# Local attention results moved into token tiles in pieces of a multiple of 16 rows and a remainder

## The chip, the cores and the metric

The kernel runs on one core of one Trainium2 chip. The metric is the device time of the core in microseconds (us). TensorE (PE) does the matrix products, VectorE (DVE), ScalarE (ACT) and GpSimd (POOL) the elementwise work, and SyncE (SP) issues every DMA of this kernel, one after the other in a fixed order; the transfers themselves run on the core's 16 DMA engines.

## The reference

Shapes: batch 8, 8 heads, 576 positions, head dimension 64; the feed-forward layer goes from 512 to 2048 and back. All in float32.

```python
# pooled attention: q, k, v averaged over groups of 4 positions, softmax over 144 positions
out_up = np.repeat(sm_attn(q_d, k_d, v_d), 4, axis=2)
# local attention: each position sees those less than 4 away
mask = np.abs(pos[:, None] - pos[None, :]) < 4
out_local = softmax(np.where(mask, scale * q @ k.T, -1e9)) @ v
x = (out_up + out_local), heads side by side          # 8 x 576 x 512
xn = (x - mean(x)) / sqrt(var(x) + 1e-6) * g_ln
return x + relu(xn @ w_ch1) @ w_ch2
```

## The kernel before, in words

The 4608 tokens (8 x 576) are 36 tiles `x` of 128 rows by 512. Two tiles make a chunk; there are 18 chunks, and each runs through the whole feed-forward layer on PE (`ffn`, L984 on): 8 pairs of hidden blocks, each pair 24 matmuls of "up" (L996, `h`) and 12 of "down" (L1019, `acc`). Products are made from a high and a low float32r part of each factor, so every product is done three times. The weights are loaded once, in 64 loads (L347, L352), and split into high and low parts by ACT and DVE (L359 to L383) in the first 150 us.

**Local attention** (`local`, L405 to L664) is done in 40 windows, 5 for each batch element. A window takes 116 output positions: two halves ("par") of NQ = 58 positions, each half with 64 keys. A window loads q, k and v (L419, L437; the first 7 windows, which are turned by PE, with L428 and L443), PE makes scores (L540), DVE masks them, ACT takes exponentials, PE turns them (`lt`, L575) and multiplies by v (`lv`, L596), and DVE divides into the window's result `xl` (L612).

**The moves.** `xl` has other rows on other partitions than the tiles `x`, so it is moved there by DMAs from SBUF to SBUF. L635 to L643 cut each half's 58 rows at the tiles' edges (every 128 tokens) into moves. A move of a window from the eighth on is two DMAs, one for each half of the heads (L662), with m partitions of 4 x 64 elements; in windows 5 and 6 it is one DMA of m rows of 512 (L659). Most of the first batch element's results are gathered by PE without a move (L884); two small moves remain at L956. In all there are 92 moves of two DMAs and 8 of one.

**The norm.** `load_up` (L865) loads the pooled result of a tile into `up`. POOL adds it to `x` (`plus`, L896) when every move into the tile has landed. DVE takes mean and variance (`st`, L904 to L907), POOL the root (L910), DVE normalises (`xn`, L914), PE turns (`px`, L923), and ACT and DVE split the turned tile into `xh` (L930) and `xlo` (L940), the inputs of the chunk's "up" matmuls.

**What sets the order.** A planner in the kernel (`Plan`, L23 to L115) lists all tasks with an engine, a cost, a due time and the buffers they take and give. It plays them through in Python while the program is built and fixes the order of every engine's instructions. At run time each engine works through its list in that order and waits where its inputs are not there. A move counts in the plan as one task of SP, with a cost of 1.52 us for two DMAs, a landing allowance LAT of 2.5 us behind it, and the buffer of `xl` comes free behind the window's last move:

```python
t = add("SP", 0.76 if by_pe else 1.52, move, outs, due + 1.0, take=() if n in piece else U,
        give=U if e == len(moves) - 1 else (), lag=LAT, kb=116)
```

Most buffers (`xl`, `x`, `up`, `xh`, `xlo`, `hh`, `hl`, weights, q and k) are the same pool of 88 units (NU). An instruction that first writes a unit waits for the last instruction or DMA that used it, whatever that was for.

Of the kernel before, what the change touches and what calls it, by code (L numbers as in the profile page):

```python
# [139 lines left out]
def attention_then_ffn(  # L140
# [258 lines left out]
    def window_start(w, par):  # L399
        return min(max(NQ * (2 * w + par) - (FACTOR - 1), 0), S - 64)  # L400
# [4 lines left out]
    def local(i):  # L405
# [230 lines left out]
        for par in range(2):  # L636
            s0 = NQ * (2 * w + par)
            n = min(NQ, S - s0)
            t, r0 = b * S + s0, s0 - window_start(w, par)
            while n:  # L640
                m = min(n, P - t % P)
                moves.append((t // P, t % P, r0, m, par))
                t, r0, n = t + m, r0 + m, n - m  # L643
        if own:
# [417 lines left out]
    for i in range(NPB * NWIN):  # L1062
        local(i)
    for b in range(B):
        pooled(b)
    for i in range(NPB * NWIN, B * NWIN):
        local(i)
# [48 lines left out]
```

## Time and profile before

| what | value |
|---|---|
| times of three runs | 1081.28, 1079.04, 1079.87 us; median 1079.87 |
| profiled execution: span from first to last instruction | 1080.9 us (no other time is given for it) |
| span against the median | 1.0 us longer |
| busy: PE, PEld, DVE, ACT, POOL | 96%, 86%, 47%, 29%, 25% |
| mean granted TensorE clock | 0.989 of full speed |
| DMA | 104.34 MB, mean 97 GB/s |

Span and runs agree within the runs' own spread. Busy shares are averages over the whole span; what a stretch waits for is read from its own rows. SP's issuing is not counted as busy; it is read from the timeline of the SP queue, where a row gives the start, the length and the number of merged issues.

### The profile page before, as it was taken

How to read it: one execution, taken by the hardware profiler on the slowest of the kernel's cores; microseconds unless marked ns; L12 is line 12 of the kernel's file. 1: busy time of each engine (PE TensorE's matmuls, PEld its weight loads, DVE VectorE, ACT ScalarE, POOL GpSimd, SP SyncE). 2: the span in 40 equal slices, each digit the busy share in tenths (PEclk: the TensorE clock that was granted, in tenths of full speed). 3: DMA queues.
4: the chain of work that ended last, by engine and by line, in shares of the span. 5: the costliest groups of instructions: out<-in, count | busy, mean ns of one | idle time of the engine just before them, and what ended most of it. 6: DMA issues, size and time to landing. Idle time of an engine off the chain costs nothing.

```text
span 1080.9 us, 23774 instructions
## 1 busy us (share of the span) xinstructions
PE 1040.3 (96%) x9290; PEld 933.6 (86%) x9290; DVE 511.9 (47%) x1309; ACT 312.7 (29%) x852; POOL 266.2 (25%) x285
## 2 busy tenths in 40 slices
PE   8987999989989999999999999999979999999998
PEld 8875898978879898989898989898968988888997
DVE  7699954434243535345344443645424353543211
ACT  5675633222222322132222221223212222222110
POOL 4234454314004221141213231142311400100000
PEclk9999899989999999999999999999999999999999
DMA  7798554625333443344343435252533333300000
GB/s 155 211 270 235 121 147 112 144 61 120 82 88 89 99 97 79 65 92 107 82 110 77 109 69 125 47 137 51 126 87 76 69 74 74 85 10 30 9 20 20
DMA packets 289296, 104.34 MB, mean 97 GB/s; under 512 B 237945, under 2 KB 276089, under 8 KB 289185
## 3 DMA queue, kind: packets, MB, share of 16 engines
q1 hardware_dynamic: 289185, 102.83, 40.2%
q8 instruction: 73, 1.20, 0.5%
q14 instruction: 38, 0.31, 0.1%
HBM read 82.58 MB, written 11.80 MB: 87 GB/s over the span
## 4 chain that ended last, share of the span: by engine, by line
PE 78%; DMA 9%; DVE 5%; SPq 4%; issue 2%; ACT 1%; POOL 1%; DVEq 0%; ACTq 0%; POOLq 0%
PE h L996 33%; PE acc L1019 32%; PE gv L802 3%; DMA s<-in_moe_w_ch_dram 2%; PE lv L596 2%; PE ls L540 2%; DMA x<-xl 2%; PE gs L766 2%; PE lt L575 1%; SPq L419 1%; PE px L923 1%; PE gt L785 1%; SPq L662 1%; DVE cva L370 1%; SPq L428 1%
## 5 line engine op out<-in xcount | busy, mean ns | idle before, releaser
L1019 PE MATMUL acc<-hi,hl 128*128 128x512 f32 x576 | 239.1, 415 | 10.2 <-DVE hl L1007 8.5
L1019 PE MATMUL acc<-lo,hh 128*128 128x512 f32 x576 | 228.5, 397 | 0.0
L1019 PE MATMUL acc<-hi,hh 128*128 128x512 f32 x576 | 226.8, 394 | 0.0
L1007 DVE SCALAR_TENSOR_TENSOR hl<-h,hh 128x512 fp32r<-128x512 f32 x144 | 98.9, 687 | 242.8 <-ACT hh L1003 222.8
L1003 ACT ACTIVATE hh<-h 128x512 fp32r<-128x512 f32 x144 | 86.1, 598 | 433.5 <-PE h L996 379.7
L996 PE MATMUL h<-xh,lo 128*128 128x256 f32 x1152 | 193.5, 290 | 0.0
L996 PE MATMUL h<-xlo,hi 128*128 128x256 f32 x1152 | 185.6, 284 | 0.0
L996 PE MATMUL h<-xh,hi 128*128 128x256 f32 x1152 | 185.6, 283 | 0.0
L996 PEld LDWEIGHTS h<-xh,lo 128*128 128x128 f32 x1152 | 169.4, 190 | 17.6 <-POOL lo L383 0.2
L996 PEld LDWEIGHTS h<-xlo,hi 128*128 128x128 f32 x1152 | 159.4, 192 | 0.0
L996 PEld LDWEIGHTS h<-xh,hi 128*128 128x128 f32 x1152 | 159.1, 192 | 0.0
L896 POOL TENSOR_TENSOR x<-x,up 128x512 f32<-128x512 f32 x32 | 41.2, 1289 | 376.8 <-DMA x<-xl 264.5
L1019 PEld LDWEIGHTS acc<-hi,hl 128*128 128x128 f32 x576 | 110.1, 191 | 27.5 <-DVE hl L1007 11.4
L1019 PEld LDWEIGHTS acc<-hi,hh 128*128 128x128 f32 x576 | 109.2, 190 | 25.3
L1019 PEld LDWEIGHTS acc<-lo,hh 128*128 128x128 f32 x576 | 110.3, 191 | 12.7
L930 ACT ACTIVATE xh<-px,gain 128x128 fp32r<-128x128 f32 x144 | 44.3, 367 | 79.5 <-PE px L923 43.6
L940 DVE SCALAR_TENSOR_TENSOR xlo<-px,gain,xh 128x128 fp32r<-128x128 f32 x144 | 43.0, 344 | 38.3 <-ACT xh L930 26.1
L904 DVE BATCH_NORM_STATS2 st<-x 128x6 f32<-128x512 f32 x32 | 22.1, 690 | 69.9 <-POOL x L896 68.7
L1027 DVE SCALAR_TENSOR_TENSOR x<-acc,x 128x512 f32<-128x512 f32 x36 | 24.3, 683 | 35.5 <-PE acc L1019 35.3
L546 DVE TENSOR_TENSOR ls<-ls,mask 128x256 f32<-128x256 f32 x66 | 27.0, 424 | 27.3 <-PE ls L540 22.3
L779 ACT ACTIVATE ag<-gs,gmx 96x144 f32<-96x144 f32 x96 | 28.8, 373 | 35.1 <-DVE gmx L771 33.1
L802 PEld LDWEIGHTS gv<-vd,agt 72*72 72x72 f32 x512 | 37.1, 145 | 1.5
(195 smaller groups left out, 1152.7 us busy)
## 6 DMA issues: line engine op xcount, KB each, us to landing
s<-in_moe_w_ch_dram SPq DMA_DIRECT2D x64, 256.0 KB
vwin<-in_v_dram SPq DMA_DIRECT2D x160, 64.0 KB
out_dram<-x SPq DMA_DIRECT2D x36, 256.0 KB
qr<-in_q_dram SPq DMA_DIRECT2D x264, 32.0 KB
kr<-in_k_dram SPq DMA_DIRECT2D x264, 32.0 KB
up<-ud SPq DMA_DIRECT2D x28, 256.0 KB
x<-xl SPq DMA_DIRECT2D x66, 58.0 KB
ud<-od SPq DMA_DIRECT2D x32, 72.0 KB
```

What stands on the lines that cost most here:

```text
L546: nc.vector.tensor_add(x.ps[n], x.ps[n], mask.unsqueeze(1).broadcast_to([P, NPAIR, 64]))
L779: nc.scalar.activation(y.a[:, c], y.ps[:, c], AF.Exp, scale=POOLED_SCALE, bias=y.mx[:, c : c + 1])
L802: nc.tensor.matmul(y.pv[:, qh, h2], lhsT=y.at[kh][:, h2, qh * GH : (qh + 1) * GH], rhs=vd[:, kh, 2 * pr + h2], start=kh == 0, stop=kh == 1,)
L896: nc.gpsimd.tensor_add(xt[n], xt[n], x.up)
L904: nc.vector.bn_stats(st, x.up if by_pe else xt[n])
L930: nc.scalar.activation(xh[c][i][:, k, j * P : (j + 1) * P], pxt[n][:, kc], AF.Copy, scale=gain[:, kc : kc + 1])
L940: nc.vector.scalar_tensor_tensor(out=xlo[c][i][:, k, ts], in0=pxt[n][:, kc], scalar=gain[:, kc : kc + 1], in1=xh[c][i][:, k, ts].bitcast(F ...
L996: nc.tensor.matmul(ph[c, p][:, fi], lhsT=wt[:, kc], rhs=xx[kc // 2][:, kc % 2], start=n == 0, stop=n == 3 * KC - 1)
L1003: nc.scalar.activation(hh[c, p], ph[c, p], AF.Relu)
L1007: nc.vector.scalar_tensor_tensor(out=hl[c, p].rearrange("p c t -> p (c t)"), in0=ph[c, p].rearrange("p c t -> p (c t)"), scalar=0.0, in1=h ...
L1019: nc.tensor.matmul(acc[c][j], lhsT=lt[:, fi, ts], rhs=rt, start=p == 0 and fi == 0 and n == 0, stop=p == NPR - 1 and fi == 1 and n == 2,)
L1027: nc.vector.scalar_tensor_tensor(out=x, in0=acc[c][j], scalar=1.0 + 2.0**-23, in1=x, op0=ALU.mult, op1=ALU.add)
```

## The change

One line is added to the loop that cuts a half's rows into moves: a piece of m rows becomes the largest multiple of 16 that is not over m; what is left is cut again in the next turn of the loop. A piece under 16 rows stays as it is.

```diff
             while n:
                 m = min(n, P - t % P)
+                m = m // 16 * 16 or m
                 moves.append((t // P, t % P, r0, m, par))
                 t, r0, n = t + m, r0 + m, n - m
```

So 58 rows become 48 and 10; 54 become 48 and 6; 34 become 32 and 2; 16 and 48 stay one piece. Moves with two DMAs go from 92 to 168, that is from 184 DMAs to 336; those with one DMA from 8 to 14. The bytes are the same. Each move is a task of the plan with the cost, the allowance and the release above, so the planner finds another order for all engines. Lines below L641 have a number higher by one in the changed kernel.

**SP, before tile 7's last moves.** `x7` is tile 7, `xl8` the result of window 8, `raw` a load for pooled attention, `kr10` and `qr10` keys and queries of window 10. Before:

```order
L700 DMA raw5v1_3028<-in_v_dram 72x4x256
L419 DMA kr10_3034<-in_k_dram 32x8x32 x4
L419 DMA qr10_2969<-in_q_dram 32x8x32 x4
L825 DMA ud2_2687<-od4_1_3082 72x2x128
L419 DMA kr10_3034<-in_k_dram 32x8x32 x4
L700 DMA raw6q0_3140<-in_q_dram 72x4x256
L700 DMA raw6k0_3143<-in_k_dram 72x4x256
L662 DMA x7_2883<-xl8_3136 58x4x64 x2
L662 DMA x7_2883<-xl8_3136 42x4x64 x2
L662 DMA x8_3175<-xl8_3136 16x4x64 x2
```

The same place in the changed kernel:

```order
L701 DMA raw5v1_3088<-in_v_dram 72x4x256
L826 DMA ud2_2709<-od4_1_3086 72x2x128
L419 DMA qr10_3016<-in_q_dram 32x8x32 x4
L701 DMA raw6q0_3146<-in_q_dram 72x4x256
L663 DMA x7_2931<-xl8_3142 48x4x64 x2
L663 DMA x7_2931<-xl8_3142 10x4x64 x2
L663 DMA x7_2931<-xl8_3142 32x4x64 x2
L663 DMA x7_2931<-xl8_3142 10x4x64 x2
L663 DMA x8_3212<-xl8_3142 16x4x64 x2
```

Eight loads of `kr10` and one of `raw6k` have moved from ahead of tile 7's moves to behind them, and the tile takes eight DMAs in place of four.

**ACT, chunk 13.** `xh13_0` and `xh13_1` are the two halves of the chunk's high part, `px26` and `px27` its turned tiles; in brackets are the semaphores for which an instruction waits (DMAHW: landings of DMAs). Before:

```order
L930 ACTIVATE xh13_0_10420<-px26_10404,gain_75 128x128 [waits PE_49,Activation_49]
L930 ACTIVATE xh13_0_10420<-px26_10404,gain_75 128x128
L930 ACTIVATE xh13_1_10438<-px26_10404,gain_75 128x128 [waits DMAHW4_49,DMAHW5_49,DMAHW1_49,DMAHW6_49,DMAHW0_49,DMAHW7_49,DVE_49,Activation_49]
L930 ACTIVATE xh13_1_10438<-px26_10404,gain_75 128x128
L930 ACTIVATE xh13_0_10420<-px27_10468,gain_75 128x128 [waits PE_49]
```

In the changed kernel:

```order
L931 ACTIVATE xh13_0_10550<-px26_10532,gain_75 128x128 [waits PE_49]
L931 ACTIVATE xh13_0_10550<-px26_10532,gain_75 128x128
L931 ACTIVATE xh13_1_10571<-px26_10532,gain_75 128x128 [waits DVE_49]
L931 ACTIVATE xh13_1_10571<-px26_10532,gain_75 128x128
L931 ACTIVATE xh13_0_10550<-px27_10602,gain_75 128x128 [waits PE_49]
```

`xh13_1` no longer waits for six DMA landings. In the same way `xlo9_0` (chunk 9) and `xlo14_0` (chunk 14) lose theirs on DVE. Over the program, the splits into `xh` and `xlo` that wait for a DMA landing go from 17 to 12; some of the 12 stand at chunks where none stood before (`xh7_0`, `xh7_1`).

**SP, among the weight loads.** `s2_13` is a weight block of the second matrix, `xl6` the result of window 6. Before:

```order
L700 DMA raw2v0_1699<-in_v_dram 72x4x256
L659 DMA x5_1315<-xl6_1693 58x512
L659 DMA x5_1315<-xl6_1693 18x512
L659 DMA x6_1741<-xl6_1693 40x512
L352 DMA s2_13_0_1760<-in_moe_w_ch2_dram 128x512
L352 DMA s2_13_1_1761<-in_moe_w_ch2_dram 128x512
```

In the changed kernel:

```order
L437 DMA vwin3_79<-in_v_dram 64x4x64 x4
L660 DMA x5_1328<-xl6_1695 48x512
L660 DMA x5_1328<-xl6_1695 10x512
L660 DMA x5_1328<-xl6_1695 16x512
L660 DMA x5_1328<-xl6_1695 2x512
L660 DMA x6_1762<-xl6_1695 32x512
L660 DMA x6_1762<-xl6_1695 8x512
L701 DMA raw2v1_1783<-in_v_dram 72x4x256
L352 DMA s2_13_0_1785<-in_moe_w_ch2_dram 128x512
L352 DMA s2_13_1_1786<-in_moe_w_ch2_dram 128x512
```

Six DMAs stand ahead of `s2_13` in place of three, and one load of `raw2v` has come between.

## Rows read from the trace of the kernel before

**Rows 1.** The page: busy engines (part 1), shares of the chain that ended last (part 4).

```profile
PE 1040.3 (96%) x9290; PEld 933.6 (86%) x9290; DVE 511.9 (47%) x1309; ACT 312.7 (29%) x852; POOL 266.2 (25%) x285
...
PE h L996 33%; PE acc L1019 32%; PE gv L802 3%; DMA s<-in_moe_w_ch_dram 2%; PE lv L596 2%; PE ls L540 2%; DMA x<-xl 2%; PE gs L766 2%; PE lt L575 1%; SPq L419 1%; PE px L923 1%; PE gt L785 1%; SPq L662 1%; DVE cva L370 1%; SPq L428 1%
```

**Rows 2.** Busy time by stretch: stretch, PE, PEld, DVE, ACT, POOL, clock, DMA share, GB/s.

```profile
600.00:700.00 100.00, 100.00 (x939) 89.99 (x938) 47.62 (x127) 25.25 (x67) 21.09 (x22) 1.00 0.38 80
700.00:800.00 100.00, 100.00 (x908) 89.98 (x908) 42.69 (x108) 23.83 (x61) 28.13 (x29) 1.00 0.44 103
```

**Rows 3.** Timeline of PE after 200 us, instructions after a pause: start, length, [pause <-releaser].

```profile
235.36 1.12 PE L575 MATMUL lt<-ident,la 128*128 128x128 f32 x4 [4.99 <-ACT la L570]
...
303.42 0.66 PE L923 MATMUL px<-ident,xn 128*128 128x128 f32 x4 [2.77 <-DVE xn L914]
...
583.18 0.66 PE L923 MATMUL px<-ident,xn 128*128 128x128 f32 x4 [1.98 <-DVE xn L914]
...
810.08 1.11 PE L923 MATMUL px<-ident,xn 128*128 128x128 f32 x4 [5.78 <-DVE xn L914]
...
868.83 0.66 PE L923 MATMUL px<-ident,xn 128*128 128x128 f32 x4 [1.21 <-DVE xn L914]
```

**Rows 4.** Chain that ended last, before the last three pauses: start, length, what.

```profile
575.55 4.91 DMA x<-xl
...
802.83 5.25 DMA x<-xl
...
808.30 0.63 ACT xh L930 x2
...
862.65 4.41 DMA x<-xl
```

**Rows 5.** Busy time by stretch while only moves are under way.

```profile
804.50:805.00 0.50, 0.00 (x0) 0.00 (x0) 0.29 (x1) 0.00 (x0) 0.50 (x2) 1.00 0.16 36
```

**Rows 6.** Busy time by stretch at the lower clock.

```profile
807.40:814.40 7.00, 4.32 (x15) 3.75 (x16) 4.61 (x12) 3.06 (x10) 0.00 (x0) 0.51 0.26 71
234.10:240.90 6.80, 5.54 (x19) 4.84 (x20) 1.69 (x3) 3.39 (x13) 0.00 (x0) 0.50 0.22 34
```

**Rows 7.** Timeline of the SP queue: start, length, line, merged issues.

```profile
104.83 2.40 SPq L659 DMA_DIRECT2D x<-xl  x3
...
219.49 7.91 SPq L662 DMA_DIRECT2D x<-xl  x6
...
571.56 5.18 SPq L662 DMA_DIRECT2D x<-xl  x6
```

**Rows 8.** Issues by line: count, min/median/max ns, first and last start us.

```profile
L662 SPq DMA_DIRECT2D x<-xl x184: 605/787/2176, 194.5 to 1001.6; - x184
...
L419 SPq DMA_DIRECT2D qr<-in_q_dram x264: 311/448/1813, 114.7 to 932.0; - x132
L419 SPq DMA_DIRECT2D kr<-in_k_dram x264: 311/448/1857, 116.8 to 934.0; - x132
...
L437 SPq DMA_DIRECT2D vwin<-in_v_dram x132: 595/615/1601, 98.5 to 907.7; - x132
```

**Rows 9.** Chain that ended last, before the pause at 235.36 us.

```profile
224.33 3.24 DMA x<-xl
...
227.73 1.30 POOL x L896
```

**Rows 10.** Timeline of DVE at L904: start, length, [idle before <-releaser].

```profile
229.05 0.69 DVE L904 BATCH_NORM_STATS2 st<-x 128x6 f32<-128x512 f32 x1 [10.55 <-POOL x L896]
...
296.67 0.69 DVE L904 BATCH_NORM_STATS2 st<-x 128x6 f32<-128x512 f32 x1 [7.73 <-POOL x L896]
...
674.86 0.69 DVE L904 BATCH_NORM_STATS2 st<-x 128x6 f32<-128x512 f32 x1 [6.16 <-POOL x L896]
...
803.07 0.69 DVE L904 BATCH_NORM_STATS2 st<-x 128x6 f32<-128x512 f32 x1 [10.53 <-POOL x L896]
```

**Rows 11.** Waits: engine line <- releaser: us in total, times, longest us.

```profile
POOL x L896 <- DMA x<-xl: 264.5, 19, 28.0
...
SPq L419 <- DVE cva L370: 3.0, 1, 3.0
```

## The prediction

> **What bounds the kernel now.** I read the page first, then stretches, then what ends each pause of PE. PE is busy for 96% of the span, and two thirds of the chain that ended last are its feed-forward products [rows 1]. In whole stretches PE never pauses, though moves run there too [rows 2]. So a late move costs nothing by itself. It costs where it makes PE pause, and where the pause is followed by a lower granted clock.
>
> After 200 us there are five pauses of over 1 us, 16.7 us in all [rows 3]. Following each back along the chain gives two kinds.
>
> *Kind A*, at 583, 810 and 868 us: 1.98 + 5.78 + 1.21 = 8.97 us. Ahead of each the chain shows a move of 4.4 to 5.3 us from its issue on [rows 4]. The instruction behind the move is not one that needs the tile: it is a write of `xh` or `xlo`. These take a unit that was `xl`, and must wait until the move has read it. At 810 us ACT writes the second half of `xh` at 808.30, when the move issued at 802.83 has landed, and DVE and PE stand behind it.
>
> *Kind B*, at 235 us: 4.99 us. Tile 7 is added up at 227.73, when a move issued at 224.33 has landed [rows 9]. DVE stood at `st` for 10.55 us [rows 10], and with it the window whose `la` PE needed. The move was late since SP reached it late: its six issues began at 219.49 [rows 7], behind the loads that the order shows.
>
> The pause at 303 us (2.77) I leave in both kernels. Two pauses bring a granted clock of one half (1.2 GHz in place of 2.4): PE worked 4.32 us so after the pause at 810 and 5.54 us after that at 235 [rows 6]. Half of that is lost: 2.2 and 2.8 us.
>
> **The change, part by part.** *How a move runs.* While only moves of 58 and 46 rows are under way, the DMA share is 0.16, that is about 2.5 of 16 engines [rows 5]. The Trainium skill (DMA: Bandwidth & Descriptors, "Why a DMA increments its semaphore by 16 and not by 1") says that a DMA is spread over the largest number of engines, up to 16, that divides its outermost size: 2 for 58 and 46, 16 for 48 and 32, 10 for 10. The trace agrees for 58 and 46; that 48 rows use all 16 no row before the change shows. By that rule the landings below would lie at their lower end, and the third that I take for the remaining waits would fall to nothing: 1072.5.
>
> *What a window pays.* Take the window with pieces of 24, 34 and 58 rows. Before: six issues from 571.56, 5.18 us long or 0.86 each [rows 7], and the last landing at 575.55 + 4.91 = 580.46 [rows 4], 8.9 us after the first issue. Afterwards: 16, 8, 32, 2, 48, 10, twelve issues. The last is issued 11 x 0.86 = 9.5 us after the first. Its landing is not in the trace. It lies between its own issue (0.86) and 3.24 us, a 42-row move behind slow ones [rows 9]: 10.3 to 12.7 us after the first issue. I take 11.5, nearer the middle because no slow piece is ahead. So the `xl` buffer comes free about 2.6 us **later** than before, not earlier; a window of 58 and 58 (eight issues, 6.0 us and then 0.86 to 3.24) comes out about even.
>
> *What the plan does with it.* The code allows 1.52 us a move and 2.5 us for the landing. For this window that was 3 x 1.52 + 2.5 = 7.1 us against 8.9 measured: the plan gave the buffer away 1.8 us too early, which is kind A. Afterwards it allows 6 x 1.52 + 2.5 = 11.6 us, about what I expect. The order bears it out: `xh13_1`, `xlo9_0` and `xlo14_0`, the three writes behind kind A, no longer wait for a landing. So **A goes: -8.97 - 2.2 = -11.1 us** (bounds 0 and -11.1). But 12 splits still wait for a landing, some at new places. Before, 17 such waits cost 11.1 us, 0.65 each; 12 at that price are 7.8 us. As the allowance now covers the landing I take a third: **+2.6** (bounds 0 and +7.8).
>
> *B.* The order puts nine loads behind tile 7's moves: eight at 0.448 [rows 8] and one like them, about 4.4 us with the gaps. It adds four issues ahead of the tile's last landing: 4 x 0.86 = 3.4. So the tile is whole about 1.0 us sooner; had the six issues taken 0.86 each in place of 7.91 / 6 = 1.32, it would be 3.7. I take 2.5 us of the pause and half of the clock's 2.8: **-3.9** (bounds 0 and -7.8).
>
> *Weights, before 150 us.* At 104.83 three moves take 2.40 us, 0.80 each [rows 7]; now six stand ahead of `s2_13`: +2.4 us, and two more pieces at an earlier place, +1.6. SP waits 3.0 us for DVE soon after [rows 11], which can hide most of it. Without that cover it is 4.0. I take half: **+2.0** (bounds 0 and +4.0).
>
> *SP from 194 to 1001 us.* 152 more issues of 0.787 us are 120 us in 807. The q, k and v loads and the moves alone take 528 x 0.448 + 132 x 0.615 + 184 x 0.787 = 463 us there [rows 8], so the queue goes from 57% to 72% by these alone, and gaps, pooled loads and stores come on top. Per tile (32 in all) it is 3.8 us more of issuing. POOL waits 19 times for moves [rows 11], mostly at no cost; PE feels it where DVE already stands at `st` for over 6 us, at four places [rows 10]. If each gets 2.8 us later, PE pays 11.2 us. The planner moves loads back to make up, as at tile 7, so I take two of four: **+5.6** (bounds 0 and +11.2).
>
> Sum: -11.1 + 2.6 - 3.9 + 2.0 + 5.6 = -4.8 us. From the span of 1080.9 us that is 1076.1, and the median of the runs is 1.0 us below the span: **1075.1 us**. What a measurement of this kernel can tell from no change is about 0.2%, 2.2 us.
>
> **Rivals.**
>
> *SP becomes what PE waits for (slower).* Each tile's moves land later by the extra issues and the planner's shifts do not make up. For it: in the window above the last landing is 2.6 us later at equal start. Against it: stretches without any pause [rows 2]. It decides from about 2.8 us at the four places of [rows 10]: 11.2 + 4.0 from the weights, with A gone but paid back by new waits of the same size: 1080.9 + 15.2 - 1.0 = 1095.1; with half of that, 1087.5. I call it 1090. The Trainium skill has a rule on this side (DMA: Bandwidth & Descriptors, "Rules for kernel authors"): many small transfers are to be joined into one, as under 64 KB the overhead rules; a piece of 58 KB is here cut into 48 and 10. On the issue side the trace agrees: a move's issue costs 0.787 us whatever its rows.
>
> *It only moves the waits (no change).* The three pauses go, the 12 waits and SP give them back: 1079.9. For it: at equal start no window's buffer is free sooner.
>
> *The spread is not set by the row count.* Then 48 rows land no faster than 58 and the split is pure issue: A stays, 1080.9 + 5.6 + 2.0 - 1.0 = 1087.5. Against it: rows 5, where three issues of 46 and 58 rows keep so few engines busy.
>
> *All gains, no cost:* 1080.9 - 11.1 - 7.8 - 1.0 = 1061.0. For it: everything added lies on SP, which is not PE.
>
> **How the numbers follow.** The forecast 1075.1 with its all-gains end: 0.46; waits only moved: 0.16; SP bound: 0.34; spread not by row count: 0.04. Faster by over 0.2%: 0.46; within: 0.16; slower: 0.34 + 0.04 = 0.38. The range goes from 1060, the all-gains case, to 1093, most of the slower rival; what lies outside is the rival's far end. Both signs have much of the chance: the forecast's own range is 1061 to 1078.
>
> **What would show it.** Right: no pause of PE ending in a wait for `xh13`, `xlo9` or `xlo14`; moves of 48 and 10 rows landing within 2 to 3 us of their issue; the clock at full speed around 810 us; a DMA share well over 0.16 while only moves run. Wrong: SP issuing without a gap over 40 us and more, POOL's waits for moves over 264.5 us in total with DVE's waits at `st` growing beyond 7 us at more than four tiles, or PE pausing for q and k loads. If the time is slower although A's pauses are gone, the term for SP is what I sized wrongly.

## The result and the profile after

| | before | changed |
|---|---|---|
| median of the runs | 1079.72 us (4 runs, 1079.04 to 1081.28) | 1070.38 us (4 runs, 1069.24 to 1071.28) |
| ratio, 95% interval | | 0.9905 [0.9891, 0.9919] |
| profiled execution: span | 1080.9 us | 1067.5 us (its own time: 1069.24) |

The changed kernel is **9.3 us faster**; 4.8 us were forecast. The two profiles lie 13.4 us apart. In the four runs of the changed kernel the time is 1.7 to 1.8 us above the span; if the same holds before, its profiled execution took some 1082.6 us, 2.9 above its median, and that of the changed kernel 1.1 below: 13.4 - 4.0 = 9.4.

The page of the changed kernel, parts 1 and 4 [rows 1]: PE is busy for as long as before, in a shorter span, and SP's issues of moves are no longer among the shares of the chain that the page lists.

```profile
PE 1040.7 (97%) x9318; PEld 934.7 (88%) x9318; DVE 506.9 (47%) x1305; ACT 317.2 (30%) x868; POOL 266.4 (25%) x285
...
PE h L997 36%; PE acc L1020 35%; PE gv L803 3%; PE lv L596 2%; PE gs L767 2%; DMA s<-in_moe_w_ch_dram 2%; PE ls L540 2%; PE lt L575 2%; PE gt L786 1%; PE px L924 1%; DMA x<-xl 1%; DVE cva L370 1%; PE ex L885 1%; PE gq L740 1%; SPq L419 1%
```

Busy time in the first 200 us and in the 800 after them (columns as in [rows 2]), of before:

```profile
0.00:200.00 200.00, 180.83 (x1745) 162.00 (x1746) 149.69 (x365) 105.35 (x292) 85.34 (x99) 0.97 0.68 174
200.00:1000.00 800.00, 782.33 (x7065) 702.24 (x7065) 346.84 (x916) 197.32 (x540) 178.99 (x184) 0.99 0.38 85
```

and of the changed kernel, with the stretch at the lower clock that answers to [rows 6]:

```profile
798.00:802.00 4.00, 4.00 (x12) 3.17 (x12) 2.41 (x6) 2.27 (x8) 0.00 (x0) 0.57 0.35 73
0.00:200.00 200.00, 181.19 (x1742) 162.29 (x1743) 148.38 (x361) 102.77 (x281) 82.76 (x97) 0.97 0.66 174
200.00:1000.00 800.00, 795.86 (x7184) 715.38 (x7183) 346.00 (x922) 205.88 (x569) 183.65 (x189) 1.00 0.39 86
```

PE works 13.5 us more of the 800, which is as much as the two spans differ. The timeline of PE, instructions after a pause [rows 3], now has these three over 0.25 us after 200 us:

```profile
575.18 0.63 PE L924 MATMUL px<-ident,xn 128*128 128x128 f32 x4 [0.93 <-DVE xn L915]
...
797.16 0.63 PE L924 MATMUL px<-ident,xn 128*128 128x128 f32 x4 [2.33 <-DVE xn L915]
...
916.69 0.63 PE L924 MATMUL px<-ident,xn 128*128 128x128 f32 x4 [0.79 <-DVE lr L602]
```

The pauses at 235, 303 and 868 us are gone, and a smaller one of 0.94 us at 360 with them; those at 583 and 810 are down to 0.93 and 2.33. SP's queue at tile 7 and at the window with pieces of 24, 34 and 58 rows [rows 7]:

```profile
219.34 7.61 SPq L663 DMA_DIRECT2D x<-xl  x10
...
563.27 8.75 SPq L663 DMA_DIRECT2D x<-xl  x12
```

and the last move of that window in the chain [rows 4]:

```profile
571.23 1.94 DMA x<-xl
```

Six issues of 5.18 us became twelve of 8.75, 3.6 us more; behind the last one's end the landing takes 1.15 us (571.23 + 1.94 against 563.27 + 8.75) in place of 3.72 (580.46 against 576.74), 2.6 us less. From the first issue to the last landing it is 9.9 us in place of 8.9. So in this window **the landings are faster, and the issuing eats more than that up**. The Trainium skill (DMA: Bandwidth & Descriptors, "Why a DMA increments its semaphore by 16 and not by 1") fits the landing: by its rule the last piece here, of 10 rows, runs on 10 engines, and the 58 rows that stood last before on 2. While SP issues the pieces, the DMA share is 0.15 on average, about the 0.16 of [rows 5]; behind the last issue it is 0.06, where before it stayed at 0.14 until the last landing. Two of these stretches in the changed kernel, and the last one in before:

```profile
564.00:571.00 7.00, 7.00 (x45) 6.24 (x44) 3.31 (x9) 1.85 (x5) 2.19 (x3) 1.00 0.15 34
572.20:573.00 0.80, 0.80 (x8) 0.76 (x7) 0.00 (x0) 0.11 (x1) 0.24 (x1) 1.00 0.06 13
576.80:580.40 3.60, 3.60 (x26) 3.34 (x25) 0.30 (x2) 0.37 (x2) 1.81 (x2) 1.00 0.14 32
```

A piece's issue is a little cheaper (0.673 us at the median, before 0.787 [rows 8]):

```profile
L663 SPq DMA_DIRECT2D x<-xl x336: 599/673/1810, 195.0 to 990.1; - x168
```

It differs with the number of rows, and the short pieces are not the cheap ones. Sorted by rows, the medians of the changed kernel's issues are 0.62 to 0.63 us for 16, 32 and 48 rows, 0.81 for 10 and 0.85 for 14; before they were 0.65 to 0.66 for 34 and 46 rows, 0.77 for 58 and about 1.2 for 18, 30 and 42.

DVE's waits at `st` are halved, and POOL's waits for moves are a little less than in [rows 11]. Of before, then of the changed kernel:

```profile
DVE st L904 <- POOL x L896: 68.7, 18, 10.5
...
POOL x L897 <- DMA x<-xl: 236.2, 19, 24.8
...
DVE st L905 <- POOL x L897: 34.5, 17, 6.4
```

Counted from the first issue, that window's last landing is thus 1.0 us later, and POOL's add of tile 7 0.7 us sooner (7.6 us, before 8.2). This is small against the waits that shrink. That made two things separate questions: the form of the DMAs, and the order that the planner finds when it counts 168 moves where there were 92.

### The profile page after: what moved, and what is told of

It reads as the page before. It is cut to its first block, busy times and chain, and to the rows that moved or that the text cites. A ratio compares the mean times of both kernels' runs of the same rounds, so it can differ in the third digit from the quotient of the medians.

```text
span 1067.5 us, 24104 instructions
## 1 busy us (share of the span) xinstructions
PE 1040.7 (97%) x9318; PEld 934.7 (88%) x9318; DVE 506.9 (47%) x1305; ACT 317.2 (30%) x868; POOL 266.4 (25%) x285
## 4 chain that ended last, share of the span: by engine, by line
PE 88%; DMA 4%; DVE 3%; SPq 2%; issue 1%; POOL 1%; ACT 1%; DVEq 0%; POOLq 0%; ACTq 0%
PE h L997 36%; PE acc L1020 35%; PE gv L803 3%; PE lv L596 2%; PE gs L767 2%; DMA s<-in_moe_w_ch_dram 2%; PE ls L540 2%; PE lt L575 2%; PE gt L786 1%; PE px L924 1%; DMA x<-xl 1%; DVE cva L370 1%; PE ex L885 1%; PE gq L740 1%; SPq L419 1%
## 5 line engine op out<-in xcount | busy, mean ns | idle before, releaser
L803 PE MATMUL gv<-vd,agt 72*72 72x65 f32 x512 | 38.8, 231 | 1.6 <-POOL mv L911 1.6
```

The costliest lines, as they stand in the source:

```text
L803: nc.tensor.matmul(y.pv[:, qh, h2], lhsT=y.at[kh][:, h2, qh * GH : (qh + 1) * GH], rhs=vd[:, kh, 2 * pr + h2], start=kh == 0, stop=kh == 1,)
```

## The experiments

In the theories, **S** is: moves on 16 engines land sooner, and that pays. **O**: the new order pays, whatever the DMAs are. The further letters say by what the order gains: **L**, that more time is allowed for the landing; **R**, that the plan keeps as much of SP's time for a move as it really takes; **D**, that any other order would be as likely to be better; **P**, that moves stand ahead of more loads on SP. The kernel before was run again beside each group of runs, with medians from 1079.72 to 1082.54 us; rows of different groups are to be compared by their ratios.

| kernel | DMAs for moves | time, us | ratio to before, 95% |
|---|---|---|---|
| changed kernel | cut | 1070.38 | 0.9905 [0.9891, 0.9919] |
| cut in the old order | cut | 1092.08 | 1.0106 [1.0084, 1.0128] |
| new order | whole | 1066.25 | 0.9870 [0.9848, 0.9892] |
| new order, 58 as 46 + 12 | cut | 1074.20 | 0.9941 [0.9921, 0.9961] |
| only slow pieces cut | some cut | 1067.71 | 0.9878 [0.9857, 0.9900] |
| landing allowance + 1.52 | whole | 1089.44 | 1.0070 [1.0047, 1.0092] |
| cost 1.44 | whole | 1084.70 | 1.0019 [0.9993, 1.0044] |
| cost 1.60 | whole | 1078.63 | 0.9971 [0.9955, 0.9987] |
| cost 2.00 | whole | 1071.93 | 0.9899 [0.9871, 0.9926] |
| cost 2.28 | whole | 1066.42 | 0.9859 [0.9827, 0.9891] |
| **cost 3.04** | whole | **1058.31** | **0.9774 [0.9727, 0.9822]** |
| cost 3.80 | whole | 1062.30 | 0.9818 [0.9802, 0.9835] |
| cost 2.28 | cut | 1080.84 | 0.9986 [0.9961, 1.0010] |
| cost 3.04 | cut | 1064.36 | 0.9850 [0.9811, 0.9889] |
| loads dearer | whole | 1072.38 | 0.9911 [0.9892, 0.9930] |
| moves due 5 us earlier | whole | 1067.18 | 0.9880 [0.9850, 0.9909] |
| moves due 13 us earlier | whole | 1091.09 | 1.0083 [1.0054, 1.0112] |
| loads behind moves, 4 us | whole | 1083.32 | 1.0022 [0.9998, 1.0045] |
| loads behind moves, 6 us | whole | 1092.87 | 1.0107 [1.0070, 1.0143] |

**The cut in the order of before.** The plan of before stays as it is; where it issues a move, the pieces are issued one after the other (also at the two other places that issue moves).

```diff
+    def cut(m):
+        out, at = [], 0
+        while at < m:
+            k = (m - at) // 16 * 16 or m - at
+            out.append((at, k))
+            at += k
+        return out
...
+                for at, k in cut(m):
+                    to = xt[n][p0 + at : p0 + at + k]
```

> The order of every engine is that of the kernel before; only each DMA of a move is issued as pieces of a multiple of 16 rows and a remainder (350 DMAs instead of 192), and the plan does not know it. Theory O (the gain comes from the new order, whose allowances fit the landings): the pauses at 583, 810 and 868 us stay or grow by some 2.6 us each, because the last piece is issued later; time 1080 to 1090. Theory S (the gain comes from moves that run on 16 engines): those pauses shrink, time 1068 to 1074. Theory Q (SP has time to spare, so extra issues cost nothing, and the spread gains nothing either): 1078 to 1082.

1092.08 us, 11 us slower than before, though every engine has its old order: S falls. Tile 25 shows how the time is lost. SP's queue, POOL's add, DVE's `st` and PE's `lt` of the window that waits, of before:

```profile
726.99 5.60 SPq L662 DMA_DIRECT2D x<-xl  x6
...
732.71 1.30 POOL L896 TENSOR_TENSOR x<-x,up 128x512 f32<-128x512 f32 x1 [6.49 <-DMA x<-xl]
...
734.04 0.69 DVE L904 BATCH_NORM_STATS2 st<-x 128x6 f32<-128x512 f32 x1 [4.07 <-POOL x L896]
...
741.68 0.60 PE L575 MATMUL lt<-ident,la 128*128 128x128 f32 x4
```

and of this run:

```profile
734.88 7.59 SPq L674 DMA_DIRECT2D x<-xl  x10
...
742.59 1.28 POOL L908 TENSOR_TENSOR x<-x,up 128x512 f32<-128x512 f32 x1 [8.02 <-DMA x<-xl]
...
743.90 0.69 DVE L916 BATCH_NORM_STATS2 st<-x 128x6 f32<-128x512 f32 x1 [9.94 <-POOL x L908]
...
749.89 1.11 PE L584 MATMUL lt<-ident,la 128*128 128x128 f32 x4 [4.36 <-ACT la L575]
```

SP comes to these moves 7.9 us later than before, the issues take 2.0 us more, and the add starts 9.9 us later. PE is only 3.9 us behind when it gets here (749.89 - 4.36 against 741.68); it ran on without a pause before and now pauses for 4.36 us. The waits at `st` grow from 68.7 to 90.7 us over the program, and between 200 and 1000 us PE works 8.0 us less.

```profile
DVE st L916 <- POOL x L908: 90.7, 24, 11.2
...
200.00:1000.00 800.00, 774.29 (x6972) 693.75 (x6971) 342.37 (x906) 195.10 (x529) 179.08 (x184) 0.99 0.38 85
```

**The new order with whole moves.** The planner counts the two parts as two tasks, but the first issues all rows and the second nothing.

```diff
-                m = min(n, P - t % P)
-                moves.append((t // P, t % P, r0, m, par))
+                whole = min(n, P - t % P)
+                moves.append((t // P, t % P, r0, whole, par))
+                if whole > 16 and whole % 16:
+                    moves.append((t // P, t % P, r0, 0, par))
```

> The order of every engine is that of the changed kernel; each move is issued whole in the place of its first piece, and the place of its remainder stays empty (192 DMAs, 58 rows in one). Theory O: 1068 to 1072, as the order is kept and SP has less to do. Theory S: back to 1078 to 1082, as the moves run on 2 engines again.

1066.25 us, better than both kernels: **the gain is the order's, and the cut takes 4 us of it back**. Apart from the moves, every engine's instructions stand in the same order as in the changed kernel. After 200 us one pause of PE over 0.25 us is left:

```profile
795.12 0.66 PE L927 MATMUL px<-ident,xn 128*128 128x128 f32 x4 [1.07 <-DVE xn L918]
```

The Trainium skill's rule that joins small transfers (DMA: Bandwidth & Descriptors, "Rules for kernel authors") points the same way as these two runs: the same order is 4 us faster with whole moves.

**The new order with 58 cut into 46 and 12.**

```diff
+                m = m - 12 if m == 58 else m // 16 * 16 or m
```

> The order and the number of DMAs are those of the changed kernel, but 58 rows are cut into 46 and 12 instead of 48 and 10. If the engines are the largest divisor up to 16, the 46 run on 2 engines again. Theory S: 1076 to 1082. Theory O: 1069 to 1073, the extra landing time of about 2 us being inside the allowance. If the spread does not depend on the divisor: the same as the changed kernel within 1 us, and landings of the same length.

1074.20 us: with the same order and as many issues, 46 rows in place of 48 in 66 DMAs cost 3.8 us. The landing is not all that changes. The issues are longer too, 252.2 us in all against 243.5 in the changed kernel. So it is not shown what a faster landing is worth by itself.

```profile
L663 SPq DMA_DIRECT2D x<-xl x336: 602/714/1610, 199.1 to 998.2; - x168
```

**Only pieces of 58, 46 and 34 rows cut.**

```diff
+                if max(k for k in range(1, 17) if m % k == 0) < 4:
+                    m = m // 16 * 16 or m
```

> Only pieces of 58, 46 and 34 rows are cut (those that 2 engines would carry); 54, 52, 42 and the like stay whole, so there are fewer DMAs, and the planner makes a third order. Theory S: 1066 to 1071, as all slow moves are gone and SP has less to do. Theory O: an order with allowances that fit about as well, 1066 to 1075. If the gain is a matter of which order was drawn: anything from 1065 to 1085.

1067.71 us, 2.7 less than the changed kernel with 74 issues fewer (262 for 336). The order is another one too, so this run does not tell issues and order apart.

**More time for the landing in the plan.** Moves whole.

```diff
-                    give=U if e == len(moves) - 1 else (), lag=LAT, kb=116)
+                    give=U if e == len(moves) - 1 else (), lag=LAT + 1.52, kb=116)
```

> Moves whole as in the kernel before; the plan's landing allowance behind a move is 4.02 us instead of 2.5, its cost on SP stays 1.52 us. Theory L (the plan gave buffers and tiles away before slow moves had landed): 1065 to 1072, the pauses behind a move's landing gone. Theory R (the plan must keep more SP time free for each move): 1076 to 1082. Theory D (which order was drawn): no telling, as likely above as below 1080.

1089.44 us: L does not explain the gain. For kind A the run speaks half against my reason, that the plan gave `xl` away 1.8 us too early. The pauses at 583 and 868 us are gone, but ahead of a pause of 6.28 us at 816 us the write of `xlo` still stands 10.23 us for a move:

```profile
812.49 0.61 DVE L940 SCALAR_TENSOR_TENSOR xlo<-px,gain,xh 128x128 fp32r<-128x128 f32 x2 [10.23 <-DMA x<-xl]
```

**The plan's cost of a move**, with whole moves: 1.44, 1.60 and 2.28 in place of 1.52. The two small steps were to show what another order does by chance; 2.28 is in the direction of what the changed kernel's plan keeps: 168 / 92 x 1.52 = 2.78 us for one old move.

```diff
-            t = add("SP", 0.76 if by_pe else 1.52, move, outs, due + 1.0, take=() if n in piece else U,
+            t = add("SP", 0.76 if by_pe else 2.28, move, outs, due + 1.0, take=() if n in piece else U,
```

> Moves whole; the plan's cost of a move is 1.44 us instead of 1.52, as small a change to the other side. Theories L and R: 1077 to 1086. Theory D: it can fall to 1070 or rise to 1090.

> Moves whole; the plan's cost of a move is 1.60 us instead of 1.52, a change of 0.08 us that should mean nothing by itself. It tells how much the time moves when only another order is drawn. Theories L and R: 1077 to 1083, with pauses of over 10 us in all after 200 us. Theory D: it can fall to 1070 or rise to 1090.

> Moves whole; the plan's cost of a move is 2.28 us, one and a half times that of before and near the mean that the changed kernel's plan keeps for the pieces of one (168 / 92 x 1.52 = 2.78 us); the allowance stays 2.5 us. Theory R: 1065 to 1072. Theory L: about the same, as a longer cost also puts off the release: 1066 to 1075. Theory D: no telling.

1084.70, 1078.63 and 1066.42 us. One number in the plan gives all of the gain without a DMA more. The small steps move the time by 0.2 to 0.3%, far less than 2.28 does. They are a weak test of D, since their orders are almost that of before: over 1290 of DVE's 1309 instructions keep their sequence, with cost 2.28 1135. In the trace of before, 192 DMAs of moves took 175.6 us of SP, so a move of two took 1.83 us on average, against the 1.52 of the plan.

**Further costs: 2.00, 3.04 and 3.80.**

> Moves whole, only the plan's cost of a move raised from 1.52 to 2.00 us, which is what a pair of move DMAs takes of SP in the trace of before (175.6 us over 192 DMAs, 0.91 us each, and the gap behind each). R (the plan has to keep the time that SP really needs for a move): 1067 to 1073 us, ratio 0.987 to 0.994, pauses of PE after 200 us under 11 us. D (the gain of 2.28 is one lucky order among many): as the draws of 1.44 and 1.60 did, 1076 to 1087 us, pauses 13 to 20 us.

> Moves whole, the plan's cost of a move 3.04 us, half as much again as SP takes. R says that time kept beyond what SP needs buys nothing: 1066 to 1072 us, no lower than 2.28 beyond the runs' spread, pauses of PE after 200 us 3 to 10 us. If more kept time goes on helping as it did from 1.52 to 2.28 (-15 us for 0.76): 1055 us or less. If too much moves the loads too late: over 1075 us, with pauses ended by q, k or v loads.

> Cost 3.80 for a whole move; a tile's last move stands ahead of 8.1 loads more. The run with 3.04 has 0.3 us of pauses left after 200 us, so there is nothing more to win there: 1054 to 1060 us if nothing turns round. If SP is now overfull in the plan and the loads of q, k and v come too late: over 1065 us, with DVE or PE waiting for those loads.

1071.93, 1058.31 and 1062.30 us. R held for 2.00 and missed for 3.04: time kept beyond the issues pays too, up to a point. From 1.52 to 3.04 the time falls with each of the five costs, and that speaks against D far more than the two small steps do. Chance is not excluded: two other orders, with the longer allowance and, below, with moves due 13 us earlier, ran 0.7 and 0.8% slower than before. Cost 3.04 **beats both kernels**, by 2.3% under before. Its stretch from 200 to 1000 us and its waits at `st`:

```profile
200.00:1000.00 800.00, 799.69 (x7212) 718.94 (x7211) 349.25 (x923) 207.49 (x572) 181.31 (x186) 1.00 0.39 85
```

```profile
DVE st L904 <- POOL x L896: 12.4, 6, 4.6
```

PE has no more to win there. At tile 7, SP's queue now has six moves from 212.58 us on, 6.9 us sooner than before, and `st` finds the tile there (221.10, no idle time ahead):

```profile
212.58 5.60 SPq L662 DMA_DIRECT2D x<-xl  x6
```

```profile
221.10 0.69 DVE L904 BATCH_NORM_STATS2 st<-x 128x6 f32<-128x512 f32 x1
```

**Cutting in orders that keep more time.** The first experiment's cut, with cost 2.28 and 3.04.

> The order of the run with cost 2.28 for all engines, and each move issued as its multiple of 16 rows and the remainder at its one place. If cutting costs what it did in the order of before, whatever the order: +11 us on 1066.4, 1077 to 1079 us. If it cost that much there only because the order kept too little of SP's time (R): 1067 to 1072 us, as the changed kernel stands 4 us above its own order with whole moves. If the faster landings pay (S): under 1066 us.

> The order of cost 3.04, which has 0.3 us of pauses after 200 us with whole moves, and each move cut at its one place. Cutting cost 11 us in the order of before and 14 in that of 2.28, 4 in the changed kernel's own. If it costs by the place where the order has no time left for it, it costs least here: 1059 to 1066 us. If it costs the same in every order that keeps the time of a whole move: 1068 to 1073 us.

1080.84 and 1064.36 us: 14 and 6 us above the same orders with whole moves (8 for the second by the ratios). The cut cost time in all four orders: 11 and 14 us where the plan kept 1.52 and 2.28 us for a whole move, 6 to 8 where it kept 3.04, and 4 in the changed kernel, whose plan kept 1.52 for each piece. That it would cost little with 2.28 was wrong.

**Loads dearer.** `DMA`, the plan's price of a q or k load and of a store, from 0.5 to 0.6 us; moves at 1.52.

```diff
-    DMA, LAT, W_AHEAD, W_LAG = 0.5, 2.5, 40, 1.5
+    DMA, LAT, W_AHEAD, W_LAG = 0.6, 2.5, 40, 1.5
```

> Moves whole at cost 1.52; instead the constant for the q and k loads and the stores goes from 0.5 to 0.6 us a DMA (the trace: 0.448). R in its wide sense (the plan needs more of SP's time kept, no matter for which DMAs): 1066 to 1074 us. If it has to be kept for the moves themselves, since only they are priced under what they take: 1076 to 1086 us.

1072.38 us: it helps as well, so the time need not be kept for the moves themselves.

**Moves due earlier.** `due + 1.0` in the line of the cost became `due - 4.0`, then `due - 12.0`.

```diff
-            t = add("SP", 0.76 if by_pe else 1.52, move, outs, due + 1.0, take=() if n in piece else U,
+            t = add("SP", 0.76 if by_pe else 1.52, move, outs, due - 4.0, take=() if n in piece else U,
```

> Moves whole, cost 1.52 as before, but due 5 us earlier in the plan: a tile's last move then stands ahead of 2.6 loads more on SP on average (tiles 6 to 33; 2.3 with cost 3.04), at other tiles than there, and no more time is kept for it. P (place: what pays is that the moves stand ahead of loads): 1058 to 1070 us, pauses of PE after 200 us under 7 us. R (kept time: what pays is that the plan lets more of SP's time pass between a move and those who need it): 1076 to 1086 us, pauses 13 to 20 us.

> As the run with the moves due 5 us earlier, but 13 us: a tile's last move stands ahead of 7.5 loads more on average. P: 1052 to 1066 us, or less good where loads now come late. R: 1076 to 1090 us.

1067.18 and 1091.09 us: the first as P says, the second against it. In the first PE works 11.5 us more than before between 200 and 1000 us:

```profile
200.00:1000.00 800.00, 793.78 (x7142) 711.30 (x7132) 346.83 (x921) 197.39 (x534) 180.70 (x186) 1.00 0.38 83
```

**Loads put behind the moves on SP alone.** After the planning, with every other engine's order as before:

```diff
+        moved = [t for t in tasks if t.kb == 116 and t.dur == 1.52]
+        for t in moved:
+            j, late = tasks.index(t), []
+            for s in tasks[j::-1]:
+                if s.end < t.open - 6.0:
+                    break
+                if s.kb == 200 and not any(s in x.deps for x in tasks[:j] if x.kb != 200):
+                    late.insert(0, s)
+            for s in late:
+                tasks.remove(s)
+            j = tasks.index(t) + 1
+            tasks[j:j] = late
```

> The same with 4 us in place of 6: 2.0 loads more on average. P: between the run with 6 us and before, 1066 to 1076 us. If the other engines' order is what pays: 1076 to 1088 us.

> The plan of before as it is, with the order of PE, DVE, ACT and POOL unchanged; only on SP the q and k loads that the plan ends less than 6 us ahead of the time at which a window's result is there are put behind that window's moves. A tile's last move then stands ahead of 3.3 loads more on average (tiles 6 to 33). P (what pays is the place of the moves on SP): 1060 to 1072 us, with the pauses of PE at 235, 303 and 868 us gone. If the other engines' order is what pays: 1076 to 1088 us. If the loads now come late: over 1082 us, with DVE or PE waiting for q and k loads.

1083.32 and 1092.87 us. With 6 us the pause at 235 is gone, but the loads pay for it: SP stands until it issues the moves of 273.28 us, `qr` follows at 278.50, DVE waits 11.71 us for it and PE 7.23. With 4 us the pause at 235 is gone as well, and new ones of 4.59 and 3.04 us stand at 213 and 287. So the moves' place on SP alone does not give the gain in the old order of the other engines; what it would be worth if no load came late these two runs do not show.

```profile
273.28 5.12 SPq L662 DMA_DIRECT2D x<-xl  x4
278.50 3.02 SPq L419 DMA_DIRECT2D qr<-in_q_dram  x4
```

```profile
287.00 0.71 DVE L499 STREAM_TRANSPOSE lqt<-qr 128x512 f32<-128x512 f32 x1 [11.71 <-DMA qr<-in_q_dram]
```

```profile
290.44 1.12 PE L575 MATMUL lt<-ident,la 128*128 128x128 f32 x4 [7.23 <-ACT la L570]
```

**How the order helps at tile 7 of the changed kernel.** DVE, in order of time:

```profile
222.67 0.55 DVE L915 TENSOR_SCALAR xn<-x,mv 128x512 f32<-128x512 f32 x1 [1.05 <-POOL mv L911]
228.22 0.69 DVE L1008 SCALAR_TENSOR_TENSOR hl<-h,hh 128x512 fp32r<-128x512 f32 x1 [5.00 <-POOL x L897]
228.82 0.42 DVE L546 TENSOR_TENSOR ls<-ls,mask 128x256 f32<-128x256 f32 x1
229.16 0.68 DVE L905 BATCH_NORM_STATS2 st<-x 128x6 f32<-128x512 f32 x1
```

POOL's add of the tile:

```profile
226.91 1.28 POOL L897 TENSOR_TENSOR x<-x,up 128x512 f32<-128x512 f32 x1 [4.27 <-DMA x<-xl]
```

and on PE the scores of the next window and its turn:

```profile
227.16 0.69 PE L540 MATMUL ls<-lkt,lqt 64*64 64x64 f32 x32
...
235.23 0.60 PE L575 MATMUL lt<-ident,la 128*128 128x128 f32 x4
```

POOL's add starts 0.8 us sooner than in [rows 9], and `st` 0.1 us later than in [rows 10] (229.16 against 229.05). But `hl` and the mask, which in before stood behind `st`, stand ahead of it, and the scores run at 227.16 us in place of 223.58: the order has put feed-forward work ahead of the window that waits. `lt` runs 0.1 us sooner than in [rows 3], and PE has not paused for it. I read this as a plan that, keeping more of SP's time, finds other work for it; that holds for this tile and is not shown for the others.

**Not settled:** which of the many moved instructions carries the gain over the whole program. A cost of SP's time in the plan gets there, for moves or for loads, and so does an earlier due time of 5 us; a longer landing, and SP's order alone, do not. The plan of the changed kernel also counts each piece with the bytes of a whole move (`kb=116`), and no run takes that apart from the time kept.

## Why the prediction was wrong in size

The direction was right: forecast 1075.1, measured 1070.38, inside the range. By terms, in the two profiles:

| term | forecast, us | measured, us |
|---|---|---|
| A with the new waits | -11.1 + 2.6 = -8.5 | pauses 8.97 to 4.05: -4.9; clock -0.4: **-5.3** |
| B | -3.9 | pause -5.0, clock -2.8: **-7.8** |
| pauses at 303 and 360 | 0 | **-3.7** |
| weights | +2.0 | some **+3.3** |
| SP | +5.6 | **0** seen |
| sum | -4.8 | -13.5 (span: -13.4) |

The clock's parts are worked as in the prediction: 4.00 us at 0.57 lose 1.7 where 4.32 at 0.51 lost 2.2; around 235 us, where before PE paused and fell to the lower clock, it keeps full speed (1.00 from 228 to 245 us). **The step that failed most is the term for SP**: 152 x 0.787 = 120 us more issuing, passed on at two of four places. The 336 issues take 243.5 us against 169.4 for the 184, 74 us more; "whatever its rows" was wrong, since the pieces of 16, 32 and 48 rows are the cheapest. And the order kept 1.52 us for each piece: the waits at `st` that were to grow became half, and no place was seen to pay. I priced the issues and left the order's answer to them at "the planner moves loads back to make up". With the old order the term would have been right in kind: there the cut cost 11 us. That the measured time lies inside the range says little: the range was 33 us wide, and the terms missed on both sides, A and the weights by 4.5 us in all too good, SP, B and the two pauses by 13.2 too bad.

*A.* Right that the order removes the waits of `xh` and `xlo` at these places; the reason is not borne out. An allowance longer by 1.52 us alone took away two of the three pauses and made the time worse. I took the pauses to vanish; two came back as 0.93 and 2.33.

*B.* The full bound came true, not half of it. The tile was whole 0.8 us sooner, near the 1.0 that I worked out, and the pause went all the same: PE worked through to `lt` without stopping. An order is more than the place of one DMA.

*303 us.* I left it in without reading what the new order does there. It went with the one at 360.

*The window of 24, 34 and 58 rows.* 11.5 us forecast from the first issue to the last landing, 9.9 measured. The issues were cheaper, 0.73 (8.75 / 12) in place of 0.86; the last piece landed 1.94 us behind the start of its issue, near the 2.0 that I took. Later than before, as forecast, by 1.0 and not 2.6.

*Weights.* PE's busy time in the first 200 us is the same, but less of it is work. L197 makes products of the identity with itself; the kernel puts them ahead of a product for which the plan lets PE wait in the first 150 us, and nothing uses their results. Their share of the first 200 us (PE and PEld busy, clock, DMA share, GB/s), of before and of the changed kernel:

```profile
0.00:200.00 200.00, 17.79 (x112) 15.54 (x112) 0.97 0.68 174
0.00:200.00 200.00, 21.44 (x140) 19.26 (x140) 0.97 0.66 174
```

The new plan sets 28 more of them. Without them PE has worked 159.8 us of 200 in place of 163.0, 3.3 us less. Sign and size fit the forecast, the reason does not: the six moves ahead of `s2_13` took 4.07 us, and yet it was issued at 106.40 us, where before the three moves of 104.83 [rows 7] ended at 107.23. The size is rough: with PE's order of before, the first experiment reaches 166.8 us of work here, and that with loads behind the moves by 6 us 162.8.

```profile
101.71 4.07 SPq L660 DMA_DIRECT2D x<-xl  x6
105.88 0.40 SPq L701 DMA_DIRECT2D raw2v<-in_v_dram  x1
106.40 0.83 SPq L352 DMA_DIRECT2D s<-in_moe_w_ch_dram  x2
```

Of my signs, two misled. The DMA share while moves run did not rise, though the landings were faster, as SP was still issuing. And the clock around 800 us fell once more, behind the pause of 2.33 us.

## What to carry to other kernels

When an edit also changes what a planner counts, run its parts singly: the new form in the old order, and the new order with the old form. Here the form cost 4 to 14 us and the order gained 14. Where a plan prices a task under what the trace shows for it (1.52 against 1.83 us on average), correct that number first, and try some values above it; here that alone gave 1058.31 us.

## What the runs showed that was not expected

The issue of a move takes another time for another number of rows, and a short piece is not always a cheap one: 0.62 to 0.63 us at the median for 16, 32 and 48 rows, 0.81 for 10, 0.77 for 58. So cutting in two costs less than twice. Faster landings did not raise the mean DMA share of a run of moves (0.15 against 0.16). And a plan that keeps well over what SP's issues take (3.04 us against 1.83) ran fastest, 8.1 us under 2.28.
